# Attention's beginning in an attention-and-two-FFN kernel: other queues, other engines and another place in the order for loads, casts, sums and scalings, and zero products tied to real ones

## The chip, the cores and the metric

The kernel runs on one core of one Trainium2 chip. The metric is the device time of one execution in microseconds (us); the time before is the median of three runs. The engines are TensorE (PE; its weight loads are listed as PEld), VectorE (DVE), ScalarE (ACT), GpSimd (POOL) and SyncE (SP, which only issues DMAs here). ACT issues some DMAs too. Each engine takes its instructions strictly in the order of its own queue, so an instruction that waits holds up all that stands behind it on that engine.

## What is computed

Three stages follow one another; the output of one is the input of the next.

```python
# 1. attention, q, k, v: (2 batches, 8 heads, 576 positions, 64)
q_d, k_d, v_d = means over groups of 4 positions          # "pooled", 144 positions
out_up    = repeat(softmax(scale * q_d @ k_d.T) @ v_d, 4)
out_local = softmax(where(|i - j| < 4, scale * q @ k.T, -1e9)) @ v
x = (out_up + out_local), as 1152 tokens x 512
# 2. a feed-forward layer: softplus(x @ w_in) @ w_out, inner width 2048
# 3. eight experts of inner width 1024, all of them for all tokens, weighted by a gate
#    whose softmax is normalised over tokens and experts eight times
```

The change touches stage 1, most of all its first 45 us.

## The kernel before, in words

**Data.** Two heads lie in one tile of 128 partitions, a *pair*; a batch has four pairs. q of a pair lies in a tile with two halves, in which the other head's rows are blanked with zeros (`blank`), so that one product of 128 rows serves one head. Batch 0's q tiles are called q0a (pairs 0 and 1) and q0b (pairs 2 and 3). v is loaded twice: `vr`, the whole v of a batch in two parts of 640 KB, to be summed in groups of four into `vd`; and `vw`, a window of 122 positions for each tile of 116 queries.

**Units.** Attention is a list of 36 units of four steps (s1 to s4). There are 16 *pooled* units (batch, half, head pair): s1 makes the scores `pd` from sums of q (`qd`, made on DVE, L249) and sums of k (`kd`, POOL L255 and L257, scaled on ACT L258), takes the maximum `nm` on DVE (L286) and the exponentials `e` on ACT (L289); s2 transposes (`ptd`, copied by ACT); s3 multiplies with `vd` (`pvd`) and divides on DVE; s4 transposes back (`pxd`). Each pooled unit of one kind needs the pairs 0 and 1, of the other kind the pairs 2 and 3. There are 20 *local* units (batch, query tile, half of the heads): s1 adds the mask (a product with a bf16 identity, L355) and the scores of q with the scaled k (`pl`, L363), s2 `ptl`, s3 `pvl`, s4 `pxl`; then DVE adds the pooled result (`xf`, L405) and POOL splits it into x (L418, L419).

**Order.** `emit` (L739) writes out the units in one list. With unit n's s1 it writes s2 of unit n-2, s3 of unit n-4 and s4 of unit n-6. Units 0 to 3 are pooled; 4 to 11 alternate local and pooled; 12 to 15 are local; then the second batch comes in. The dictionary `at` hangs other work in front of a unit: loads of batch 1 before unit 1, its v and the first weights before unit 9, its sums before units 11 to 14, and `prep` of the first weight tiles before units 14, 18, 23 and 29. `prep` turns weights given as 64-bit numbers into two 32-bit parts; one takes three passes over 128x1024 on ACT (L123, L125, L130), six on DVE (L126 to L134) and one product on POOL (L136). The weights' buffers (`raw`, two of them) are the ones in which `vr` lies first.

**Who sets the order on an engine.** The framework's planner turns this program into one queue per engine: of the instructions that it believes ready, it takes the one that stands first in the program. An instruction with no input is ready at once and so floats ahead. `tc.issue_after(ins)` holds what is traced inside the block behind `ins`, on the engine of `ins` alone, and it is an order in the queue, not a wait.

**Zero products.** `warm` (L194) issues products of a blanked tile, `pz`, whose result nobody reads: WARM = 17 at the start, then one after each of the first 19 steps, and one after each fourth step up to the 84th, 53 in all.

**Lines to follow.** Loads of q and k L239 and L243 (q of batch 0 on ACT's queue, all else on SP's); identity and mask L91 and L96, their casts L93 and L97; `vr` L273, its sums L276 and L278 (batch 0 on DVE, batch 1 on POOL); scaling of k L259; weights L107.

Of the kernel before, what the change touches and what calls it, by code (L numbers as in the profile page):

```python
# [21 lines left out]
P = 128  # L22
POOLF = 4
G = S // POOLF
GH = G // 2
# [26 lines left out]
WARM, JALL, JN, NJ = 17, 20, 4, 88  # L52
# [23 lines left out]
class Net:  # L76
# [10 lines left out]

    def constants(self):
        nc = self.nc
        self.ident = self.const.tile([P, P], F32, name="ident")  # L90
        nc.sync.dma_start(out=self.ident, in_=self.a["ident"])  # L91
        self.identb = self.atp.tile([P, P], BF16, tag="identb", name="identb", bufs=1)
        nc.vector.tensor_copy(self.identb, self.ident)  # L93
        self.mask = self.atp.tile([P, len(OFF), KW], BF16, tag="mask", name="mask", bufs=1)
        self.maskf = self.convp.tile([P, len(OFF), KW], F32, tag="cm", name="maskf", bufs=1)
        nc.sync.dma_start(out=self.maskf, in_=self.a["mask"])  # L96
        nc.vector.tensor_copy(self.mask, self.maskf)  # L97
        self.ones = self.const.tile([P, P], F32, name="ones")
        nc.gpsimd.memset(self.ones, 1.0)
# [105 lines left out]
    def attention_pools(self, stack):  # L205
        tc = self.tc
        self.convp = stack.enter_context(tc.tile_pool(name="conv", bufs=1, side="right"))
        self.qkp = stack.enter_context(tc.tile_pool(name="qkp", bufs=NPAIR, side="right"))
        self.vwp = stack.enter_context(tc.tile_pool(name="vwp", bufs=3, side="right"))
        self.atp = stack.enter_context(tc.tile_pool(name="atp", bufs=3, side="right"))  # L210
        self.tmp = stack.enter_context(tc.tile_pool(name="tmp", bufs=2, side="right"))
        self.psm = stack.enter_context(tc.tile_pool(name="psm", bufs=2, space=bass.MemoryType.PSUM))
        self.psa = stack.enter_context(tc.tile_pool(name="psa", bufs=6, space=bass.MemoryType.PSUM))
        self.kT, self.qd, self.kd, self.vw, self.vd, self.upT = {}, {}, {}, {}, {}, {}

    def places(self):


        q = self.hp.tile([P, 2, 2, S], F32, tag="h", name="q0a")
        x = self.xyp.tile([P, 2, 2, S], F32, tag="xy", name="q0b")  # L220
        self.qT = {(0, p): (q, x)[p // 2][:, p % 2] for p in range(NPAIR)}
        for t in (q, x):
            self.blank(t, self.nc.vector)
# [5 lines left out]
    def load_qk(self, b, p):  # L229
# [11 lines left out]
        for g in range(2):  # L241
            rows = slice(g * D, (g + 1) * D)
            (nc.scalar if b == 0 else nc.sync).dma_start(out=self.qT[b, p][rows, g], in_=self.a["q"][b, p][rows])  # L243

    def pool_qk(self, b, p):
# [11 lines left out]
        nc.gpsimd.tensor_tensor(kd, s[:, :, 0], s[:, :, 1], ALU.add)  # L257
        nc.scalar.activation(kd, kd, AF.Copy, scale=SCALE / (POOLF * POOLF))  # L258
        nc.scalar.activation(k, k, AF.Copy, scale=SCALE)  # L259
        self.qd[b, p], self.kd[b, p] = qd, kd  # L260

# [5 lines left out]
    def load_vd(self, b):  # L267
# [3 lines left out]
        for hf in range(2):  # L271
            r = self.rawp.tile([GP, POOLF, DM], F32, tag="raw", name=f"vr{b}{hf}")
            nc.sync.dma_start(out=r, in_=self.a["vp"][b, hf].rearrange("p (f d) -> p f d", f=POOLF))  # L273
            s = self.convp.tile([GH, 2, DM], F32, tag=("ch", "cs")[hf], name=f"vs{b}{hf}", bufs=1)
# [4 lines left out]
        self.vd[b] = vd  # L279
        self.upT[b] = self.atp.tile([P, NPAIR, G], F32, tag="upT", name=f"upT{b}", bufs=2)  # L280

    def softmax_exp(self, ps, n, m, k, tag):

        nc = self.nc
        nm = self.atp.tile([m, n], F32, tag="nm" + tag, name="nm")
        nc.vector.tensor_reduce(out=nm, in_=ps, op=ALU.max, axis=AX.X, negate=True)  # L286
        e = self.atp.tile([m, n, k], F32, tag="e" + tag, name="e", bufs=3 if tag == "l" else 2)
        for j in range(n):
            nc.scalar.activation(e[:, j], ps[:, j], AF.Exp, bias=nm[:, j : j + 1])  # L289
        return e  # L290

    def pooled(self, b, hf, p):
# [4 lines left out]
        def s1():  # L297
            ps = self.psa.tile([P, 512], F32, tag="a", name="pd")[:GH, : 2 * G].rearrange("p (j k) -> p j k", j=2)
            for j in range(2):
                nc.tensor.matmul(  # L300
# [8 lines left out]
        def s2():  # L309
# [3 lines left out]
            for j in range(2):  # L313
                for kh in range(2):
                    nc.tensor.transpose(ps[:, j, kh], st["e"][:, j, kh * GH : (kh + 1) * GH], ident[:GH, :GH])
# [4 lines left out]
        def s3():  # L320
            ps = self.psa.tile([P, 512], F32, tag="a", name="pvd")[:GH, : 2 * DA].rearrange("p (j d) -> p j d", j=2)
            for j in range(2):
                for kh in range(2):
                    nc.tensor.matmul(
# [14 lines left out]
        def s4():  # L339
            ps = self.psa.tile([P, 512], F32, tag="a", name="pxd")[:, :GH]  # L340
            nc.tensor.transpose(ps, st["ul"].rearrange("p j d -> p (j d)"), ident[:GH, :GH])
# [4 lines left out]
    def local(self, b, t, g):  # L346
# [6 lines left out]
        def s1():  # L353
            ps = self.psa.tile([P, 512], F32, tag="a", name="pl")[:nq, : 4 * KW].rearrange("p (j k) -> p j k", j=4)
            nc.tensor.matmul(  # L355
# [6 lines left out]
            for j in range(4):  # L362
                nc.tensor.matmul(  # L363
# [8 lines left out]
        def s2():  # L372
            ps = self.psa.tile([P, 512], F32, tag="a", name="ptl")[:KW, : 4 * nq].rearrange("p (j q) -> p j q", j=4)
            for j in range(4):
                nc.tensor.transpose(ps[:, j], st["e"][:, j], ident[:nq, :nq])  # L375
# [4 lines left out]
        def s3():  # L380
            ps = self.psa.tile([P, 512], F32, tag="a", name="pvl")[:nq, : 4 * DA].rearrange("p (j d) -> p j d", j=4)
            for j in range(4):
                nc.tensor.matmul(  # L383
# [12 lines left out]
        def s4():  # L396
            ps = self.psa.tile([P, 512], F32, tag="a", name="pxl")[:, : 2 * nq].rearrange("p (j q) -> p j q", j=2)
            for j in range(2):
                nc.tensor.transpose(
# [314 lines left out]
    def run(self):  # L714
# [13 lines left out]
        self.load_qk(0, 1)  # L728
        self.pool_qk(0, 0)
        self.pool_qk(0, 1)  # L730
        for p in (2, 3):
            self.load_qk(0, p)
            self.pool_qk(0, p)
        self.constants()
# [4 lines left out]
        def emit(items, rest):  # L739
# [4 lines left out]
            for it in [*items, *tail]:  # L744
# [5 lines left out]
                for k, u in enumerate(live[::STEP]):  # L750
                    if u is not None:
                        u[k]()
                        n += 1
                        if n < JALL or n % JN == 0 and n < NJ:
                            self.warm(1)
# [11 lines left out]
        def load_rest():  # L767
            self.load_vd(1)
            self.load_raw(1)
# [9 lines left out]
        at = {1: [load_second], 9: [load_rest]}  # L779
        for p in range(NPAIR):  # L780
            at.setdefault(11 + p, []).append(lambda p=p: self.pool_qk(1, p))
        for n, lag, u in zip(range(2 * NFT), (1, 1, 0, 0), (14, 18, 23, 29)):
# [212 lines left out]
```

## Time and profile before

| | us |
|---|---|
| median of three runs | 1072.9 (1071.02 to 1073.95) |
| span of the profiled execution, first to last instruction | 1069.6 |
| TensorE busy in the span | 1048.9 (98%) |
| VectorE busy | 784.1 (73%) |
| ScalarE busy | 435.1 (41%) |
| GpSimd busy | 170.3 (16%) |

Of the profiled execution the page gives no other time than its span. How to read it: a product's busy time contains its way through the array, so products that follow one another overlap in time, and a stretch in which PE is "busy" can be one in which little is done; the distance from one end to the next says more. The granted clock is the share of 2.4 GHz at which PE ran; 0.5 is 1.2 GHz. In a timeline, the bracket behind a row is the idle time of the engine before it and what ended it.

### The profile page before, as it was taken

To read this page: it belongs to the slowest core of one execution; us is meant where nothing else is said; L and a number is where in the kernel's file an instruction comes from. 1 tells how busy PE (TensorE), PEld (TensorE's weight loads), DVE (VectorE), ACT (ScalarE), POOL (GpSimd) and SP (SyncE) were. 2 spreads that over 40 slices of the span, in tenths; PEclk is the share of its full clock that TensorE was granted. 3 is DMA by queue.
4 is the path that set the end of the run, shared out by engine and by line. 5 is a ranking of instruction groups with operands and counts; after the bars stand their busy time and mean duration, and the time that the engine had idled before them with its cause. 6 is when DMAs were issued, how large, how long until landed. Compare 5 with 4: busy or idle time off the path is not lost.

```text
span 1069.6 us, 16125 instructions
## 1 busy us (share of the span) xinstructions
PE 1048.9 (98%) x6421; PEld 961.4 (90%) x6421; DVE 784.1 (73%) x1466; ACT 435.1 (41%) x815; POOL 170.3 (16%) x218
## 2 busy tenths in 40 slices
PE   7899999999999999999999999999999999999998
PEld 4899999999998899898989989898998989899896
DVE  6798799999987697784947658484765848576572
ACT  4787687766743433141413314141331414133130
POOL 3555300002012220211202011120201112020000
PEclk9899999999999999999999999999999999999999
DMA  9541032222111221111211111121111112110003
GB/s 262 165 136 61 2 119 79 79 79 79 41 40 40 79 80 40 40 41 40 79 40 40 41 40 40 40 80 40 40 40 40 41 40 79 40 40 1 1 2 88
DMA packets 13035, 63.99 MB, mean 60 GB/s; under 512 B 1760, under 2 KB 2016, under 8 KB 6496
## 3 DMA queue, kind: packets, MB, share of 16 engines
q1 hardware_dynamic: 12320, 61.79, 17.7%
q10 hardware_dynamic: 640, 1.18, 0.4%
q8 instruction: 50, 0.82, 0.3%
q14 instruction: 25, 0.20, 0.1%
HBM read 60.60 MB, written 2.36 MB: 59 GB/s over the span
## 4 chain that ended last, share of the span: by engine, by line
PE 87%; DVE 4%; ACT 3%; POOL 1%; issue 0%; ACTq 0%; DVEq 0%
PE po L585 37%; PE pu L536 32%; PE ph L443 8%; PE py L485 7%; PE pvl L383 1%; PE pl L363 0%; ACT cm L125 0%; ACT e L454 0%; DVE ch L129 0%; POOL x L418 0%; ACT r L457 0%; DVE a L167 0%; PE ptl L375 0%; ACT e L453 0%; PE pg L634 0%
## 5 line engine op out<-in xcount | busy, mean ns | idle before, releaser
L536 PE MATMUL pu<-T,a 128*128 128x320 f32 (+1 forms) x2688 | 354.1, 293 | 1.2 <-DVE yp L497 1.2
L536 PEld LDWEIGHTS pu<-T,a 128*128 128x128 f32 x2688 | 351.2, 188 | 2.7 <-issue 1.4
L585 PE MATMUL po<-w,h 128*128 128x512 f32 x960 | 225.3, 394 | 0.0
L607 DVE SCALAR_TENSOR_TENSOR acc<-po,prob,acc 128x512 f32<-128x512 f32 x126 | 94.1, 749 | 176.8 <-PE po L585 176.8
L585 PEld LDWEIGHTS po<-w,h 128*128 128x128 f32 x960 | 180.0, 188 | 41.3
L187 ACT CAST w<-raw 128x1024 fp32r<-128x1024 f32 x32 | 33.3, 1049 | 274.9 <-PE po L585 274.9
L585 PE MATMUL po<-w,h0a 128*128 128x512 f32 x576 | 142.4, 391 | 0.6 <-DVE w L188 0.6
L156 POOL TENSOR_TENSOR s<-raw 128x256 f32<-128x256 f32 x32 | 29.1, 909 | 679.5 <-DVE a L167 476.2
L585 PEld LDWEIGHTS po<-w,h0a 128*128 128x128 f32 x576 | 107.3, 188 | 22.5 <-DVE w L188 1.0
L443 PE MATMUL ph<-x,w 128*128 128x384 f32 x576 | 104.5, 337 | 1.3 <-ACT yp L495 1.3
L485 PE MATMUL py<-h,w 128*128 128x384 f32 x576 | 104.5, 338 | 1.2 <-DVE h L464 0.9
L485 PEld LDWEIGHTS py<-h,w 128*128 128x128 f32 x576 | 100.5, 188 | 1.9 <-DVE h L464 1.3
L443 PEld LDWEIGHTS ph<-x,w 128*128 128x128 f32 x576 | 100.1, 188 | 1.6 <-ACT yp L495 1.6
L548 ACT ACTIVATE h<-c 128x320 fp32r<-128x320 f32 x128 | 58.6, 469 | 79.9 <-DVE c L559 79.9
L549 DVE SCALAR_TENSOR_TENSOR h<-c,h 128x320 fp32r<-128x320 f32 x128 | 68.0, 539 | 0.3
L559 DVE TENSOR_TENSOR c<-v,pu 128x256 f32<-128x256 f32 (+1 forms) x128 | 57.7, 450 | 10.8 <-PE pu L536 7.9
L548 ACT ACTIVATE h0a<-c 128x256 fp32r<-128x256 f32 x96 | 37.4, 417 | 50.2 <-DVE c L559 50.1
L188 DVE TENSOR_TENSOR w<-raw,w 128x1024 fp32r<-128x1024 f32 x32 | 39.0, 1220 | 22.4 <-ACT w L187 22.4
L585 PE MATMUL po<-w,h0b 128*128 128x512 f32 x192 | 54.4, 390 | 0.0
L585 PEld LDWEIGHTS po<-w,h0b 128*128 128x128 f32 x192 | 36.0, 188 | 7.5
L557 ACT COPY p<-pu 128x256 f32<-128x256 f32 (+1 forms) x64 | 25.1, 393 | 37.4 <-PE pu L536 36.1
L549 DVE SCALAR_TENSOR_TENSOR h0a<-c,h0a 128x256 fp32r<-128x256 f32 x96 | 39.0, 419 | 0.9 <-ACT h0a L548 0.6
(141 smaller groups left out, 1249.3 us busy)
## 6 DMA issues: line engine op xcount, KB each, us to landing
raw<-in_w SPq DMA_DIRECT2D x48, 1024.0 KB, 4.9
vw<-in_vw SPq DMA_DIRECT2D x10, 260.0 KB, 2.8
vr<-in_vp SPq DMA_DIRECT2D x4, 640.0 KB, 8.6
k<-in_k SPq DMA_DIRECT2D x8, 288.0 KB, 5.4
out<-acc SPq DMA_DIRECT2D x5, 256.0 KB, 2.0
q<-in_q SPq DMA_DIRECT2D x8, 144.0 KB, 5.3
out<-acc SPq DMA_DIRECT2D x8, 128.0 KB, 2.3
q0a<-in_q ACTq DMA_DIRECT2D x4, 144.0 KB, 5.2
```

Of the source, the lines that this page charges most:

```text
L156: nc.gpsimd.tensor_tensor(s[:, 0], a21, a22, ALU.add)
L187: nc.scalar.copy(w[:, 0], raw)
L188: nc.vector.tensor_tensor(w[:, 1], raw, split(w[:, 0]), ALU.subtract)
L443: nc.tensor.matmul(ps[:, i], lhsT=wv[:, a, k, fo : fo + P], rhs=x[:, b, k], start=(n == 0), stop=(n == 3 * KD - 1),)
L485: nc.tensor.matmul(ps[:, a], lhsT=w[:, i, d * P : (d + 1) * P], rhs=h[:, j, f], start=(n == 0), stop=(n == 3 * NFT - 1),)
L536: nc.tensor.matmul(ps, lhsT=w[:, x, a, k], rhs=t[:, y, b, k], start=(m == 0), stop=(m == 5))
L548: act = nc.scalar.activation(hi, src, AF.Relu)
L549: dve = nc.vector.scalar_tensor_tensor(lo, src, 0.0, split(hi), ALU.max, ALU.subtract)
L557: nc.scalar.copy(to, ps)
L559: nc.vector.tensor_tensor(to, src, ps, ALU.add)
L585: nc.tensor.matmul(ps, lhsT=self.h[s, i, f][:, at * P : (at + 1) * P], rhs=w[:, j], start=(n == 0), stop=(n == 3 * NFT - 1),)
L607: nc.vector.scalar_tensor_tensor(acc, ps, pe, acc, ALU.mult, ALU.add)
```

## The change

- Loads: in the order of use. q of pair 0 stays on ACT's queue, q of the pairs 1 to 3 moves to SP's. The identity is loaded after pair 1, the mask after pair 3.
- The blanking of q0b moves from DVE to POOL, and so do the two casts to bf16 (identity, mask); these casts and the blanking of `ones` stand behind POOL's sum of k of pair 1.
- `pool_qk` of batch 0's pairs 2 and 3 moves behind the maximum (on DVE) and the exponentials (on ACT) of unit 1. The scaling of k is a function of its own, `scale_k`; batch 0's four come behind these exponentials too.
- The sums of v of batch 0 move behind the maximum of unit 3 (`sum_vd`, before unit 4).
- WARM goes from 17 to 22; each of the other 36 zero products is queued behind the real product or transpose that precedes it in the program.
- The first two `prep` move from units 14 and 18 to 16 and 19.

```diff
 STEP = 2
-WARM, JALL, JN, NJ = 17, 20, 4, 88
+WARM, JALL, JN, NJ = 22, 20, 4, 88
 GP = 80
...
+    def load_ident(self):
+        self.ident = self.const.tile([P, P], F32, name="ident")
+        self.nc.sync.dma_start(out=self.ident, in_=self.a["ident"])
+
+    def load_mask(self):
+        self.maskf = self.convp.tile([P, len(OFF), KW], F32, tag="cm", name="maskf", bufs=1)
+        self.nc.sync.dma_start(out=self.maskf, in_=self.a["mask"])
+
     def constants(self):
         nc = self.nc
-        self.ident = self.const.tile([P, P], F32, name="ident")
-        nc.sync.dma_start(out=self.ident, in_=self.a["ident"])
         self.identb = self.atp.tile([P, P], BF16, tag="identb", name="identb", bufs=1)
-        nc.vector.tensor_copy(self.identb, self.ident)
+        nc.gpsimd.tensor_copy(self.identb, self.ident)
         self.mask = self.atp.tile([P, len(OFF), KW], BF16, tag="mask", name="mask", bufs=1)
-        self.maskf = self.convp.tile([P, len(OFF), KW], F32, tag="cm", name="maskf", bufs=1)
-        nc.sync.dma_start(out=self.maskf, in_=self.a["mask"])
-        nc.vector.tensor_copy(self.mask, self.maskf)
+        nc.gpsimd.tensor_copy(self.mask, self.maskf)
         self.ones = self.const.tile([P, P], F32, name="ones")
...
         self.psa = stack.enter_context(tc.tile_pool(name="psa", bufs=6, space=bass.MemoryType.PSUM))
-        self.kT, self.qd, self.kd, self.vw, self.vd, self.upT = {}, {}, {}, {}, {}, {}
+        self.kT, self.qd, self.kd, self.vw, self.vd, self.upT, self.vr = {}, {}, {}, {}, {}, {}, {}
...
         self.qT = {(0, p): (q, x)[p // 2][:, p % 2] for p in range(NPAIR)}
-        for t in (q, x):
-            self.blank(t, self.nc.vector)
+        for t, engine in ((q, self.nc.vector), (x, self.nc.gpsimd)):
+            self.blank(t, engine)
...
             rows = slice(g * D, (g + 1) * D)
-            (nc.scalar if b == 0 else nc.sync).dma_start(out=self.qT[b, p][rows, g], in_=self.a["q"][b, p][rows])
+            (nc.scalar if b == p == 0 else nc.sync).dma_start(out=self.qT[b, p][rows, g], in_=self.a["q"][b, p][rows])
...
         kd = self.atp.tile([P, G], F32, tag="kd", name=f"kd{b}{p}", bufs=NPAIR)
-        nc.gpsimd.tensor_tensor(kd, s[:, :, 0], s[:, :, 1], ALU.add)
+        self.pooled_k = nc.gpsimd.tensor_tensor(kd, s[:, :, 0], s[:, :, 1], ALU.add)
         nc.scalar.activation(kd, kd, AF.Copy, scale=SCALE / (POOLF * POOLF))
-        nc.scalar.activation(k, k, AF.Copy, scale=SCALE)
         self.qd[b, p], self.kd[b, p] = qd, kd
+
+    def scale_k(self, b, p):
+        k = self.kT[b, p]
+        self.nc.scalar.activation(k, k, AF.Copy, scale=SCALE)
...
             nc.sync.dma_start(out=r, in_=self.a["vp"][b, hf].rearrange("p (f d) -> p f d", f=POOLF))
+            self.vr[hf] = r
+        self.vd[b] = vd
+        self.upT[b] = self.atp.tile([P, NPAIR, G], F32, tag="upT", name=f"upT{b}", bufs=2)
+
+    def sum_vd(self, b):
+        nc, vd = self.nc, self.vd[b]
+        for hf in range(2):
+            r = self.vr[hf]
             s = self.convp.tile([GH, 2, DM], F32, tag=("ch", "cs")[hf], name=f"vs{b}{hf}", bufs=1)
...
             e.tensor_tensor(vd[:, hf, :, 0:D], sv[:, 0], sv[:, 1], ALU.add)
-        self.vd[b] = vd
-        self.upT[b] = self.atp.tile([P, NPAIR, G], F32, tag="upT", name=f"upT{b}", bufs=2)
...
         nm = self.atp.tile([m, n], F32, tag="nm" + tag, name="nm")
-        nc.vector.tensor_reduce(out=nm, in_=ps, op=ALU.max, axis=AX.X, negate=True)
+        self.top = nc.vector.tensor_reduce(out=nm, in_=ps, op=ALU.max, axis=AX.X, negate=True)
         e = self.atp.tile([m, n, k], F32, tag="e" + tag, name="e", bufs=3 if tag == "l" else 2)
         for j in range(n):
-            nc.scalar.activation(e[:, j], ps[:, j], AF.Exp, bias=nm[:, j : j + 1])
+            self.exp = nc.scalar.activation(e[:, j], ps[:, j], AF.Exp, bias=nm[:, j : j + 1])
         return e
...
-                nc.tensor.matmul(
+                self.pe = nc.tensor.matmul(
...
         self.load_qk(0, 1)
+        self.load_ident()
+        self.load_qk(0, 2)
+        self.load_qk(0, 3)
+        self.load_mask()
         self.pool_qk(0, 0)
         self.pool_qk(0, 1)
-        for p in (2, 3):
-            self.load_qk(0, p)
-            self.pool_qk(0, p)
-        self.constants()
+        with self.tc.issue_after(self.pooled_k.ins):
+            self.constants()
         self.load_vd(0)
...
                         if n < JALL or n % JN == 0 and n < NJ:
-                            self.warm(1)
+                            with self.tc.issue_after(self.pe.ins):
+                                self.warm(1)
...
             self.load_vd(1)
+            self.sum_vd(1)
             self.load_raw(1)
...
-        at = {1: [load_second], 9: [load_rest]}
+        def pool_rest():
+            with self.tc.issue_after(self.top.ins), self.tc.issue_after(self.exp.ins):
+                self.pool_qk(0, 2)
+                self.pool_qk(0, 3)
+                for p in range(NPAIR):
+                    self.scale_k(0, p)
+
+        def sum_first():
+            with self.tc.issue_after(self.top.ins):
+                self.sum_vd(0)
+
+        at = {1: [load_second], 2: [pool_rest], 4: [sum_first], 9: [load_rest]}
         for p in range(NPAIR):
-            at.setdefault(11 + p, []).append(lambda p=p: self.pool_qk(1, p))
-        for n, lag, u in zip(range(2 * NFT), (1, 1, 0, 0), (14, 18, 23, 29)):
+            at.setdefault(11 + p, []).extend(
+                (lambda p=p: self.pool_qk(1, p), lambda p=p: self.scale_k(1, p))
+            )
+        for n, lag, u in zip(range(2 * NFT), (1, 1, 0, 0), (16, 19, 23, 29)):
             at.setdefault(u, []).append(lambda n=n, lag=lag: prep(n, lag))
```

## Rows read from the trace of the kernel before

**Rows 1.** The page's heading and part 1: busy time, share, instructions

```profile
span 1069.6 us, 16125 instructions
PE 1048.9 (98%) x6421; PEld 961.4 (90%) x6421; DVE 784.1 (73%) x1466; ACT 435.1 (41%) x815; POOL 170.3 (16%) x218
```

**Rows 2.** Windows: busy PE, PEld, DVE, ACT, POOL; granted clock, DMA share, GB/s

```profile
10.00:20.00 10.00, 6.73 (x43) 4.07 (x43) 6.82 (x10) 3.38 (x10) 0.95 (x3) 1.00 1.03 280
...
24.00:41.00 17.00, 16.36 (x169) 15.74 (x168) 13.03 (x35) 11.60 (x40) 10.87 (x12) 0.96 0.84 247
41.00:50.00 9.00, 6.54 (x42) 6.20 (x41) 5.15 (x14) 7.24 (x19) 1.50 (x3) 0.62 0.13 49
50.00:100.00 50.00, 46.42 (x416) 44.33 (x416) 46.83 (x120) 41.11 (x110) 30.48 (x28) 1.00 0.36 117
...
320.00:1069.60 749.60, 744.35 (x4384) 670.51 (x4383) 503.04 (x1002) 217.04 (x418) 93.58 (x120) 1.00 0.13 45
```

**Rows 3.** Windows, zero products pz alone: busy PE, their number, clock, DMA

```profile
8.00:24.00 16.00, 8.15 (x28) 0.93 1.05 276
24.00:70.00 46.00, 0.00 (x0) 0.91 0.53 165
70.00:76.00 6.00, 0.77 (x2) 1.00 0.16 44
```

**Rows 4.** Timeline of DVE, 11 to 23 us: start, length, line, instruction, idle before

```profile
11.07 0.35 DVE L97 CAST mask<-maskf 128x366 bf16<-128x366 f32 x1 [0.40 <-DMA maskf<-in_mask]
11.51 1.35 DVE L249 TENSOR_REDUCE qd<-q0b 128x288 f32<-128x1152 f32 x1
12.78 0.81 DVE L286 TENSOR_REDUCE nm<-pd 72x2 f32<-72x288 f32 x2
...
18.19 1.22 DVE L276 TENSOR_TENSOR vs<-vr 72x1024 f32<-72x1024 f32 x1 [1.90 <-DMA vr<-in_vp]
19.33 1.34 DVE L249 TENSOR_REDUCE qd<-q0b 128x288 f32<-128x1152 f32 x1
20.59 0.68 DVE L278 TENSOR_TENSOR vd<-vs 72x512 f32<-72x512 f32 x1
...
21.77 0.81 DVE L286 TENSOR_REDUCE nm<-pd 72x2 f32<-72x288 f32 x2
```

**Rows 5.** Timeline of PE, 15 to 27 us

```profile
15.95 1.46 PE L203 MATMUL pz<-z 128*128 128x512 bf16 x6
...
20.73 0.71 PE L300 MATMUL pd<-kd,qd 128*72 128x144 f32 x4 [3.31 <-DVE qd L249]
...
23.96 1.16 PE L324 MATMUL pvd<-vd,ptds 72*72 72x65 f32 x8
...
24.92 0.82 PE L300 MATMUL pd<-kd,qd 128*72 128x144 f32 x4
...
25.82 0.68 PE L324 MATMUL pvd<-vd,ptds 72*72 72x65 f32 x8
```

**Rows 6.** Timeline, 34 to 54 us: the first weights, ScalarE's wait, the products behind it

```profile
34.57 2.66 SPq L107 DMA_DIRECT2D raw<-in_w  x2
...
37.98 0.22 ACT L342 COPY upT<-pxd 128x72 f32<-128x72 f32 x1
...
40.88 1.12 ACT L125 ACTIVATE cm<-raw 128x1024 f32<-128x1024 f32 x1 [2.69 <-DMA raw<-in_w]
...
43.62 0.57 PE L355 MATMUL pl<-mask,identb 116*116 116x488 bf16 x1 [2.46 <-ACT e L289]
...
43.98 1.02 PE L363 MATMUL pl<-k,q0a 128*116 128x122 f32 x4
...
50.74 0.58 PE L363 MATMUL pl<-k,q0a 128*116 128x122 f32 x4
...
53.76 0.58 PE L363 MATMUL pl<-k,q0a 128*112 128x122 f32 x4
```

**Rows 7.** Timeline: a GpSimd cast, GpSimd's first sum of batch 1's v, a load's issue

```profile
94.17 3.34 POOL L418 CAST x<-xf 128x232 fp32r<-128x232 f32 x1 [1.74 <-DVE xf L405]
...
32.19 4.67 POOL L276 TENSOR_TENSOR vs<-vr 72x1024 f32<-72x1024 f32 x2 [1.07 <-DVE qd L249]
...
6.80 0.47 ACTq L243 DMA_DIRECT2D q0b<-in_q  x1
```

**Rows 8.** One line each: length min/median/max in ns, first and last start

```profile
L418 POOL CAST x<-xf x24: 243/376/3339, 39.7 to 127.5; 128x232 fp32r<-128x232 f32 x12, 128x224 fp32r<-128x224 f32 x4, 128x72 fp32r<-128x72 f32 x2, 128x160 fp32r<-128x160 f32 x2
L227 POOL MEMSET q<- x8: 571/572/572, 1.1 to 5.4; 64x576 f32 x8
```

More of the change, by code (lines that the diff above doesn't have):

```diff
@@ L314, in s2 @@
                 for kh in range(2):
-                    nc.tensor.transpose(ps[:, j, kh], st["e"][:, j, kh * GH : (kh + 1) * GH], ident[:GH, :GH])
+                    self.pe = nc.tensor.transpose(ps[:, j, kh], st["e"][:, j, kh * GH : (kh + 1) * GH], ident[:GH, :GH])
             pt = self.atp.tile([GH, 2, 2, GH], F32, tag="ptd", name="ptds")
@@ L323, in s3 @@
                 for kh in range(2):
-                    nc.tensor.matmul(
+                    self.pe = nc.tensor.matmul(
                         ps[:, j],
@@ L340, in s4 @@
             ps = self.psa.tile([P, 512], F32, tag="a", name="pxd")[:, :GH]
-            nc.tensor.transpose(ps, st["ul"].rearrange("p j d -> p (j d)"), ident[:GH, :GH])
+            self.pe = nc.tensor.transpose(ps, st["ul"].rearrange("p j d -> p (j d)"), ident[:GH, :GH])
             nc.scalar.copy(self.upT[b][:, p, hf * GH : (hf + 1) * GH], ps)
@@ L354, in s1 @@
             ps = self.psa.tile([P, 512], F32, tag="a", name="pl")[:nq, : 4 * KW].rearrange("p (j k) -> p j k", j=4)
-            nc.tensor.matmul(
+            self.pe = nc.tensor.matmul(
                 ps,
@@ L362, in s1 @@
             for j in range(4):
-                nc.tensor.matmul(
+                self.pe = nc.tensor.matmul(
                     ps[:, j],
@@ L374, in s2 @@
             for j in range(4):
-                nc.tensor.transpose(ps[:, j], st["e"][:, j], ident[:nq, :nq])
+                self.pe = nc.tensor.transpose(ps[:, j], st["e"][:, j], ident[:nq, :nq])
             pt = self.atp.tile([KW, 4, nq], F32, tag="ptl", name="ptls")
@@ L382, in s3 @@
             for j in range(4):
-                nc.tensor.matmul(
+                self.pe = nc.tensor.matmul(
                     ps[:, j], lhsT=st["pt"][:, j], rhs=self.vw[b, t][:KW, 4 * g + j], start=True, stop=True
@@ L398, in s4 @@
             for j in range(2):
-                nc.tensor.transpose(
+                self.pe = nc.tensor.transpose(
                     ps[:, j], st["ul"][:, 2 * j : 2 * j + 2].rearrange("p j d -> p (j d)"), ident[:nq, :nq]
```

## Prediction

> **What bounds the kernel now.** I read the busy times first, then the windows, then the timelines of the stretches where PE stands idle. The span is PE's: 98% busy, and from 320 us on 744 of 750 us [rows 1, 2]. Nothing of the change lies there. The windows show where time without real products can still lie: 10 to 20 us, where PE's busy 6.73 us are largely zero products while DMA is saturated (share 1.03, 280 GB/s); then 41 to 50 us, where PE is busy 6.54 of 9 us at a mean granted clock of 0.62. From 24 to 41 us only 0.64 us of PE are idle, from 50 to 100 us 3.6, and there DVE has 46.8 of 50 us filled [rows 2]. So after the start PE is the bound, and each thing put into its queue costs what it takes, unless a wait swallows it.
>
> The start's chain stands in DVE's timeline: the first maxima (nm) come at 12.78, behind the mask's cast and a sum of q of pair 2; the sum of pair 3 comes only at 19.33, behind a sum of v that waited 1.90 us for its load; the second maxima follow at 21.77 [rows 4]. On PE the scores of pair 3 wait for it 3.31 us, till 20.73, and the first pvd starts at 23.96; from there PE runs closely [rows 5]. The stop at 41 us is ACT's: it waits 2.69 us for the first weights, the exponentials stand behind, PE waits 2.46 us and goes on at 1.2 GHz: four pl take 1.02 us, and 0.58 us later at 2.4 GHz [rows 6].
>
> **The change, part by part.**
>
> 1. **q's sums ahead of v's.** Pair 3's sum (1.34 us) [rows 4] no longer stands behind a sum of v; maxima, exponentials and transposes of the first four units are then done before `vd` is. What is late next is `vd` itself: the same loads (four k, eight q, identity, mask, two parts of v; 3.8 MB by their shapes) stand ahead of v's second part, and DMA was saturated, so it still lands at about 18.1. Behind it 1.22 us of sum and 0.68 of the next make 20.1 [rows 4], and the first pvd follows: 23.96 - 20.1 = 3.9 us earlier. The other vs and vd stand in DVE's queue in front of the first local maxima; that wait of DVE is the old one without the 1.34 us. I add 0.6 us for products that PE can put ahead of vd (one group of pd, some transposes, at the distances of [rows 5]): **-4.5**. Bounds: -1.3 (vd's own gain, the sum of q gone from between) and -6 (the first scores of a local unit, 1.0 us as two groups of 0.58 that overlap [rows 6], done ahead too).
>
> 2. **Clock at the start.** From 24 to 41 us the clock is 0.96, so some 1.4 us are at 1.2 GHz, and the first pvd takes 1.16 us against 0.68 later [rows 2, 5]. With no long wait in front: **-0.5** (bounds -0.7 and 0).
>
> 3. **Zero products.** The trace has 28 of them between 8 and 24 us, none from 24 to 70, two after [rows 3]: without inputs they floated ahead and filled waits. One costs (1.46 - 0.38)/5 = 0.217 us of PE [rows 3, 5], 0.38 being the length of one, 0.77/2. Tied, they stand behind their steps. Steps 9 to 19 come after the first pvd (it is step 9), that is 11, and of the 17 later ones 15 are new there: 26 x 0.217 = 5.6 us at most. The waits left hide some: 0.64 us in 24 to 41 us, and a part of the 3.6 us in 50 to 100 us [rows 2]. I take 18 of them before 41 us less 0.64, that is 3.3, and 0.4 after: **+3.7** (bounds 0, if all fall in waits, and 5.6). WARM's five more replace those that used to float to the start; they lie in the wait for the first loads and cost nothing; if the first scores came earlier than they end, 1.1 us.
>
> 4. **prep two units later.** The first weights' buffers are v's of batch 1: their load is issued at 34.57, behind GpSimd's first sum of it at 32.19 (two sums, 4.67 us), and ACT gets them at 40.88 [rows 6, 7]. All this hangs on saturated DMA and does not move. ACT came to the place at 38.2 [rows 6]. By parts 1 to 3 (zero products with the 3.3 us that fall before) it comes 1.7 us earlier, 36.5, and two local units later: 50.74 to 53.76, 3.0 us each [rows 6], so at 42.5. The load has landed: PE's 2.5 us of wait go, and with them the low clock. At 0.62 over 9 us 6.8 us were at 1.2 GHz [rows 2]; some 5 us of that had products, half is lost: 2.4 us. **-4.9** (bounds -5.4, with ACT's smaller waits, and +1.7, if ACT stops at the same place and waits for the same landing: then what was won before is used up).
>
> 5. **Moves of queues and engines.** Six issues of q, 0.47 us each [rows 7], go from ACT to SP; SP then has 12 issues ahead of v's, some 5.6 us, before anything but DMA's own pace decides: 0 (bounds 0 and +0.5). The two blankings on GpSimd take about 2 x 1.14 us, from 0.57 us for half the width [rows 8], ahead of its sums of k; covered by vd, which comes later in any case; without that cover 2.3 us. ACT's four scalings of k stand behind the exponentials of unit 1 and in front of the first pl; hidden by the same cover: 0 (bounds 0 and +1). The mask is loaded after pair 3, and GpSimd waits for it with the casts in front of what comes next on its queue, sums of k of batch 1, needed far later: 0. A GpSimd cast has a median of 0.38 us but took 3.34 us in the stretch where DVE is full [rows 7, 8]; that would put the first pl 3.0 us later, still before vd's 20.1. The Trainium skill (SBUF — State Buffer, Who interferes with whom) says more sharply that a DVE operation with two SBUF inputs and a GpSimd one that reads SBUF block each other wholly, and a tensor_reduce never does, so a cast beside v's sums would wait for a whole sum; by that rule this part would be +1, by the rows' cover 0, and the row of 3.34 us agrees with it as far as one row can.
>
> 6. **Given back later.** DVE is 94% full from 50 to 100 us [rows 2], and its work on the weights can't begin before they land. At 41 us attention is ahead by 1.7 us, so PE's gain above that must come from DVE's slack of 3.2 us in 50 to 100 and 3.9 in 41 to 50. I take back **+2.1** (bounds 0 and 4.9, all of part 4).
>
> Sum: -4.5 - 0.5 + 3.7 - 4.9 + 0 + 2.1 = **-4.1 us**. Against the profiled span of 1069.6 [rows 1] this is 1065.5; the runs' median is 3.3 us above that span, and I keep the distance: **1068.8 us**, 0.4% less. About 0.3% (3.2 us) is what a measurement of this kernel can tell from no change.
>
> **Rivals.**
>
> *The landing pins everything (no change).* The planner places ACT's work on the weights where it believes them landed, not where the program has unit 16; if that is the same place relative to attention, ACT waits for the same landing at 40.88 and PE's gain is gone by 43.6. For it: the landing is DMA's, and a tie orders, it doesn't wait. Against: the program's order decides among what is ready, and units 14 and 15 now come first. Left is parts 1 to 3 absorbed, plus the zero products after unit 13, 10 less two old ones, 1.7 us at most, partly in waits: +0.6, 1073.5 us.
>
> *Zero products cost more than the start gains (slower).* Place: PE's queue behind steps 9 to 84; price 5.6 us by part 3. It decides, with ACT's wait kept at its old length, once the first pvd comes later than 23.96 - (5.6 - 3.2) = 21.6 us. With the start at its lower bound (-1.3): +4.3, 1077.2 us. For it: the closeness of PE from 24 us on. Against: 2.5 + 3.6 us of waits in which they can lie.
>
> *The start doesn't move*, because GpSimd, now with blankings, casts and sums of k in one queue, holds up the sums of k of pairs 2 and 3: vd covers it unless it is over 5 us; then parts 1 and 2 fall away and the sum is +0.9, 1073.8 us.
>
> **Chances.** Forecast 0.52, landing 0.27, start unmoved 0.06, zero products 0.15. The forecast's own range is 1064.5 to 1070.5: parts 1 and 6 at their better ends below, 3 and 6 towards their worse ends above. The whole range goes on to 1074.0, to take in both cases of no change; above it lie the slower rival and little else. Faster by over 0.3%: 0.50 (the forecast, less its upper end, and a little of the landing's case with a shorter wait); the same 0.34; slower 0.16.
>
> **What would show it.** Step 1: nm of units 0 and 1 before 11 us, the sum of pair 3 before the sums of v, pvd first at about 20. Step 2: clock 1.0 from 20 to 41 us. Step 3: some 26 pz from 20 to 70 us, PE's waits shorter beside them. Step 4: no ACT row that waits over 1 us for the weights, clock 1.0 in 41 to 50 us, first weights' pass at 41 to 43 us. Step 5: GpSimd's mask cast before 16 us. Step 6: DVE still over 90% in 50 to 100 us. I am wrong if ACT waits again for the weights' landing, if pvd does not start before 22 us, or if the time is won or lost after 150 us.

## The result and the profile after

The changed kernel takes **1083.1 us** (median of six, 1080.18 to 1085.9); the kernel before, beside it, 1072.9. The ratio is 1.0103 [1.0084, 1.0122]: 1.0% **slower**, where 0.4% faster was forecast. The profiled execution was the slowest of the six (1085.9), so its spans, 1084.1 against 1069.6, lie 4 us further apart than the medians.

The heading and part 1 of the page, for [rows 1]:

```profile
span 1084.1 us, 16121 instructions
PE 1055.8 (97%) x6426; PEld 968.1 (89%) x6426; DVE 783.0 (72%) x1462; ACT 435.6 (40%) x815; POOL 172.7 (16%) x222
```

PE is busy 7 us more, of a span 14.5 longer; GpSimd, which took over casts and a blanking, is busy 2.4 us more, DVE and ACT as before. The windows, for [rows 2] (columns as there):

```profile
10.00:20.00 10.00, 6.62 (x32) 5.34 (x33) 3.43 (x4) 5.14 (x14) 2.97 (x8) 0.54 1.04 277
24.00:41.00 17.00, 12.48 (x99) 10.91 (x99) 9.90 (x25) 6.46 (x21) 8.49 (x6) 0.80 0.84 228
41.00:50.00 9.00, 7.94 (x45) 6.28 (x45) 1.72 (x5) 7.32 (x20) 1.75 (x4) 0.62 0.17 69
50.00:100.00 50.00, 48.02 (x433) 45.21 (x433) 46.59 (x116) 40.16 (x111) 26.79 (x31) 1.00 0.31 97
100.00:120.00 20.00, 16.80 (x123) 16.07 (x122) 12.44 (x32) 10.38 (x30) 8.26 (x7) 0.83 0.21 67
```

Three things: PE is less busy from 24 to 41 us (12.48 us, before 16.36) and at a lower clock (0.80, before 0.96); DVE has 1.72 us of work in the nine from 41 to 50 (before 5.15 [rows 2]); and 50 to 100 us are full as before, so there is little room to catch up. The zero products, for [rows 3]:

```profile
8.00:24.00 16.00, 2.92 (x6) 0.68 1.04 276
24.00:70.00 46.00, 9.92 (x25) 0.85 0.48 139
```

The start, for [rows 4, 5]: first GpSimd and ACT, then DVE and PE, from the timeline:

```profile
3.01 4.90 POOL L231 MEMSET q<- 64x576 f32 x8
8.01 1.28 POOL L259 TENSOR_TENSOR ks<-k 128x288 f32<-128x288 f32 x2
...
13.07 2.39 ACT L267 ACTIVATE k<-k 128x576 f32<-128x576 f32 x4
...
15.36 0.53 ACT L262 ACTIVATE kd<-kd 128x144 f32<-128x144 f32 x2
...
22.36 0.68 ACT L267 ACTIVATE k<-k 128x576 f32<-128x576 f32 x1 [4.02 <-POOL ks L259]
...
25.10 0.68 ACT L267 ACTIVATE k<-k 128x576 f32<-128x576 f32 x1 [2.06 <-POOL ks L259]
...
25.69 1.16 ACT L302 ACTIVATE e<-pd,nm 72x144 f32<-72x144 f32 x4
```

```profile
10.08 1.02 PE L313 MATMUL pd<-kd,qd 128*72 128x144 f32 x6 [2.69 <-ACT kd L262]
11.13 0.45 DVE L299 TENSOR_REDUCE nm<-pd 72x2 f32<-72x288 f32 x1 [1.71 <-PE pd L313]
...
12.41 2.60 DVE L253 TENSOR_REDUCE qd<-q0b 128x288 f32<-128x1152 f32 x2
...
15.72 0.75 PE L313 MATMUL pd<-kd,qd 128*72 128x144 f32 x2 [3.30 <-ACT kd L262]
...
20.06 0.45 DVE L299 TENSOR_REDUCE nm<-pd 72x2 f32<-72x288 f32 x1 [5.05 <-PE pd L313]
...
26.11 0.72 PE L328 MATMUL ptd<-ident,e 72*72 72x72 f32 x4 [4.18 <-ACT e L302]
...
27.48 0.43 PE L337 MATMUL pvd<-vd,ptds 72*72 72x65 f32 x2
```

q's sums do stand ahead of v's (12.41, both in a row), but the scores come no earlier. Three other waits took the place of the old one: the blankings of batch 1's q, now themselves behind q0b's, stand ahead of GpSimd's first sum of k (8.01, before 6.11); ACT's four scalings of k stand ahead of kd of pairs 2 and 3 (15.36); and batch 1's scalings of k, which wait for GpSimd's sums of the same k and through them for a load, stand ahead of the exponentials of units 2 and 3 (25.69). The first pvd starts at 27.48, 3.5 us **later** than before [rows 5]. Around 40 us, for [rows 6, 7]:

```profile
32.17 2.35 POOL L291 TENSOR_TENSOR vs<-vr 72x1024 f32<-72x1024 f32 x1 [7.10 <-DMA vr<-in_vp]
...
35.94 2.35 POOL L291 TENSOR_TENSOR vs<-vr 72x1024 f32<-72x1024 f32 x1 [1.41 <-DVE qd L253]
...
38.25 2.48 POOL L293 TENSOR_TENSOR vd<-vs 72x512 f32<-72x512 f32 x2
40.70 0.80 POOL L261 TENSOR_TENSOR kd<-ks 128x144 f32<-128x144 f32 x2
41.15 0.32 ACT L262 ACTIVATE kd<-kd 128x144 f32<-128x144 f32 x1 [5.20 <-POOL kd L261]
...
42.06 1.24 PE L313 MATMUL pd<-kd,qd 128*72 128x144 f32 x4 [3.48 <-ACT e L302]
43.13 1.12 ACT L127 ACTIVATE cs<-raw 128x1024 f32<-128x1024 uint32 x1
43.40 0.46 DVE L299 TENSOR_REDUCE nm<-pd 72x2 f32<-72x288 f32 x1 [4.01 <-PE pd L313]
```

The wait of 2.69 us for the first weights is gone (cs at 43.13 waits for nothing). But ACT waits 5.20 us for kd of batch 1's first pairs, with exponentials behind it, PE 3.48 us for these, DVE 4.01. In the trace of before, GpSimd's same sums are done much earlier:

```profile
29.07 0.81 POOL L257 TENSOR_TENSOR kd<-ks 128x144 f32<-128x144 f32 x2 [5.27 <-PE pd L300]
```

There they stand **ahead** of the sums of batch 1's v [rows 7], in the changed kernel behind them. The first part of v lands at 32 us in both, and its sums are 2 x 2.35 + 2.48 = 7.2 us of GpSimd, so what stands behind them cannot run before some 39 us; as the second part's sum starts only at 35.94, it is 40.70. Near 110 us PE stops once more, this time for the fourth weight tile, its clock at 0.83 in that window:

```profile
108.22 2.66 POOL L140 TENSOR_TENSOR w<-cs,ch 128x1024 fp32r<-128x1024 f32 x1
...
110.93 0.69 PE L498 MATMUL py<-h,w 128*128 128x384 f32 x1 [3.11 <-POOL w L140]
```

Read by the end of the same product in both traces, the changed kernel is 5.5 us behind at the 32nd pvd (35.4 us), 14.0 at the 32nd pd (51.1), 8.8 at the 72nd pl (60.5), 9.7 at the 80th pvl (79.2), 14.3 at the 120th pvl (121.0), and from there the distance stays. Of the 14.0, 5.2 come back because the kernel before has its own stop and low clock behind its 32nd pd [rows 6], which the changed one has not. About two thirds of the loss, then, are there once the stop at 42 us is over, and 4.6 us come at the stop near 110. That the second stop follows from the first is not shown: the fourth tile's product starts 9.8 us later than before (98.42), hardly more than PE is late by then.

### The profile page after: what moved, and what is told of

Read it like the earlier page. It is cut to its first block, busy times and chain, and to the rows that moved or that the text cites. A ratio compares the mean times of both kernels' runs of the same rounds, so it can differ in the third digit from the quotient of the medians.

```text
span 1084.1 us, 16121 instructions
## 1 busy us (share of the span) xinstructions
PE 1055.8 (97%) x6426; PEld 968.1 (89%) x6426; DVE 783.0 (72%) x1462; ACT 435.6 (40%) x815; POOL 172.7 (16%) x222
## 4 chain that ended last, share of the span: by engine, by line
PE 86%; DVE 4%; ACT 2%; POOL 1%; issue 0%; DVEq 0%; ACTq 0%
PE po L598 37%; PE pu L549 32%; PE ph L456 8%; PE py L498 7%; PE pvl L396 1%; PE pl L376 1%; DVE ch L133 0%; ACT cm L129 0%; ACT r L470 0%; ACT e L467 0%; DVE cs L137 0%; DVE a L171 0%; ACT w L134 0%; PE pg L647 0%; DVE T L539 0%
```

## The experiments

Each ratio is to the kernel before on the same chip (median 1072.1 to 1073.7). "First pvd" and DVE's work from 10 to 50 us are from the profiles.

| kernel | us | ratio | first pvd, us | DVE 10 to 50, us |
|---|---|---|---|---|
| before | 1072.9 | 1 | 23.96 | 27.58 |
| changed | 1083.1 | 1.0103 [1.0084, 1.0122] | 27.48 | 18.12 |
| e1 loads, casts, blanking | 1067.8 | 0.9951 [0.9937, 0.9965] | 22.34 | 27.21 |
| e2 sums, scalings | 1071.8 | 0.9984 [0.9964, 1.0003] | 21.69 | 29.03 |
| e3 ties | 1079.1 | 1.0059 [1.0038, 1.0081] | 24.48 | 29.87 |
| e4 prep later | 1070.1 | 0.9964 [0.9941, 0.9986] | 25.36 | 27.18 |
| e5 changed, untied | 1073.7 | 1.0013 [1.0002, 1.0023] | 24.10 | 23.05 |
| e6 changed, k before v | 1072.8 | 1.0006 [0.9991, 1.0020] | 27.41 | 24.62 |
| e7 changed, k scaled later | 1083.3 | 1.0107 [1.0088, 1.0126] | 23.64 | 18.24 |
| e8 changed, old sums | 1072.0 | 0.9998 [0.9985, 1.0011] | 23.08 | 26.38 |
| e9 e1 and e4 | 1066.9 | 0.9955 [0.9942, 0.9968] | 22.77 | 28.52 |
| e10 e9, k scaled later | 1069.6 | 0.9981 [0.9966, 0.9995] | 22.83 | 27.85 |
| e11 e5, e6 and e7 | 1070.5 | 0.9990 [0.9973, 1.0006] | 22.43 | 24.07 |
| e12 e6, 17 pz fewer | 1071.7 | 0.9989 [0.9973, 1.0005] | 27.04 | 24.95 |
| e13 changed, start mended | 1080.5 | 1.0079 [1.0059, 1.0099] | 23.11 | 20.56 |
| e14 e13 and e6 | 1075.9 | 1.0039 [1.0025, 1.0053] | 23.10 | 25.79 |
| e15 e1, q blanked later | 1070.9 | 0.9994 [0.9982, 1.0006] | 18.65 | 27.27 |
| e16 e1 again | 1068.1 | 0.9962 [0.9946, 0.9977] | 23.07 | 27.17 |

### Each part alone

**e1**: the kernel before with the loads' order, and the casts and q0b's blanking on GpSimd.

```diff
-        for t in (q, x):
-            self.blank(t, self.nc.vector)
+        for t, engine in ((q, self.nc.vector), (x, self.nc.gpsimd)):
+            self.blank(t, engine)
...
+        self.load_ident()
+        self.load_qk(0, 2)
+        self.load_qk(0, 3)
+        self.load_mask()
```

> The kernel before with the loads' order, the casts and the blanking of q0b on GpSimd alone. Queues theory (the loss comes when batch 1's sums of v on GpSimd, waiting for their load, get ahead of batch 1's sums of k, and ScalarE and TensorE wait for these): here GpSimd keeps the sums of k first, so 1070 to 1076 us. Start theory (GpSimd comes to the first sums of k 2 us late, TensorE stands idle and its clock falls from 10 us on, and that alone is handed on): 1076 to 1081 us. Zero-product theory (the tied products cost 4 to 6 us): no change, 1071 to 1075 us.

Measured: 0.49% faster, below all three forecasts, and 0.38% in e16. The first pd is late (its group ends 2.2 us later), but the 16th pd comes 3.0 us earlier and the first pvd 1.6. GpSimd keeps kd ahead of v. By the ends of the same products, though, only 0.9 us of the profile's gain of 2.7 are there at the 96th py (145 us); 1.6 come right behind it, from a stop that the kernel before has and e1 and e16 have not:

```profile
146.94 8.75 PE L443 MATMUL ph<-x,w 128*128 128x384 f32 x48 [1.30 <-ACT yp L495]
```

Why it goes is not shown.

**e2**: the new places of the sums and scalings alone.

```diff
-        at = {1: [load_second], 9: [load_rest]}
+        at = {1: [load_second], 2: [pool_rest], 4: [sum_first], 9: [load_rest]}
```

> The kernel before with only the new places of the sums of q, the scalings of k and the sums of v. Queues theory: GpSimd keeps batch 1's sums of k ahead of its sums of v, so 1068 to 1075 us. Start theory: the first scores come as before, so the same or faster, 1068 to 1073. Zero-product theory: no loss, 1068 to 1073. My own prediction's first part: 1068.5, since the first pvd comes at about 20 us instead of 24.

The first pvd comes 2.3 us earlier, behind vd; at the end of the profile 0.8 us are left, and the interval holds 1: the 1068.5 of the prediction's first part did not come.

**e3**: WARM = 22 and the tie alone.

```diff
-                            self.warm(1)
+                            with self.tc.issue_after(self.pe.ins):
+                                self.warm(1)
```

> The kernel before with the zero products tied and 22 at the start, nothing else. Zero-product theory: some 26 products of 0.22 us newly on TensorE's path and gaps unfilled: 1076 to 1081 us. Queues theory: hardly any loss, since the other engines' queues stay as they were: 1071 to 1075 us.

0.59% slower, the time of the zero-product theory. But most of the loss isn't where the products stand: behind by 1.9 us at the 72nd pl (54 us) and by 1.4 at the 80th pvl (71 us), the kernel is 5.1 us behind at the 120th pvl (112 us), with a stop of 3.02 us in between. GpSimd, DVE and PE in its timeline:

```profile
99.24 2.65 POOL L136 TENSOR_TENSOR w<-cs,ch 128x1024 fp32r<-128x1024 f32 x1
...
100.19 2.11 DVE L464 TENSOR_TENSOR h<-l,h 128x384 fp32r<-128x384 f32 x1
...
102.36 0.44 PE L485 MATMUL py<-h,w 128*128 128x384 f32 x1 [3.02 <-DVE h L464]
```

DVE's h starts beside GpSimd's product of the weights and ends 0.4 us after it: 2.11 us for what takes 0.54 at its shortest, and PE waits for it. In e4, e5 and e9 h takes 2.0 us in the same way and PE waits only 0.5 us, so a long h alone does not make this stop.

**e4**: `prep` later alone.

```diff
-        for n, lag, u in zip(range(2 * NFT), (1, 1, 0, 0), (14, 18, 23, 29)):
+        for n, lag, u in zip(range(2 * NFT), (1, 1, 0, 0), (16, 19, 23, 29)):
```

> The kernel before with the first two weight tiles prepared before units 16 and 19 instead of 14 and 18. My prediction's part 4 by itself: ScalarE's wait of 2.69 us for the weights and TensorE's 2.46 us behind it go, with the low clock: 1068 to 1071 us. If the planner puts the work where it thinks the weights landed: 1071.5 to 1074.5 us. If VectorE's queue is the bound from 50 to 100 us, later weights cost: 1074 to 1078 us.

0.36% faster, a time inside the first forecast, but not for its reason: ACT still waits for the first weights, 4.38 us, and PE 4.15 us for ACT.

By their ratios times 1073 us the four alone come to -5.3 - 1.7 + 6.3 - 3.9 = **-4.6 us**; together they gave +11.1. What costs is that they meet.

### What meets what

**e5**: the changed kernel with the zero products free again and WARM = 17 (the edit of e3 taken back).

```diff
-WARM, JALL, JN, NJ = 22, 20, 4, 88
+WARM, JALL, JN, NJ = 17, 20, 4, 88
...
-                            with self.tc.issue_after(self.pe.ins):
-                                self.warm(1)
+                            self.warm(1)
```

> The changed kernel with its zero products free again (17 at the start, no ties). If the tie costs what it cost alone (6 us): 1077 us. If the parts add up (loads -5, sums -2, prep -4): 1063 us. Queues theory: here too GpSimd's queue has batch 1's sums of v ahead of its sums of k, but ScalarE's queue has the exponentials ahead of the scalings that wait for them, so most of the loss goes: 1065 to 1073 us.

**e8**: the changed kernel without the new places of sums and scalings (the edit of e2 taken back).

```diff
-        at = {1: [load_second], 2: [pool_rest], 4: [sum_first], 9: [load_rest]}
+        at = {1: [load_second], 9: [load_rest]}
```

> The changed kernel with the sums of q, the scalings of k and the sums of v where they were (so loads, casts, ties and prep changed). If the parts add up: 1073.5 - 5 + 6 - 4 = 1070 us. If it is the new places of sums and scalings together with the ties that makes the loss: also 1068 to 1073. If ties together with the loads' order make it: 1078 to 1084 us.

Either one taken back brings nearly all of the 10 us back (e5, at 1073.7, is just above its third forecast; e8, at 1072.0, fits its first two, which it cannot tell apart). In e5 GpSimd still has v's sums ahead of kd, but they come earlier, and ACT goes on at 37.61:

```profile
37.53 0.82 POOL L261 TENSOR_TENSOR kd<-ks 128x144 f32<-128x144 f32 x2
37.61 1.13 ACT L127 ACTIVATE cs<-raw 128x1024 f32<-128x1024 uint32 x1 [4.34 <-POOL vd L293]
```

So this order does not cost 10 us wherever it stands. **e6** touches neither edit; it puts batch 1's sums of v behind GpSimd's first two sums of k of batch 1. (The load of the first weights moves with them in the program; in both builds it is issued as the first sum of v ends, at 34.55 and 37.10 us.)

```diff
             self.load_vd(1)
-            self.sum_vd(1)
+
+        def sum_second():
+            with self.tc.issue_after(self.pooled_k.ins):
+                self.sum_vd(1)
             self.load_raw(1)
...
+        at[12].append(sum_second)
```

> The changed kernel with batch 1's sums of v on GpSimd behind the sums of k of its pair 1. Queues theory: the scaled sum of k comes at about 35 us instead of 41, TensorE's wait of 3.5 us and the low clock after it go, and VectorE's empty stretch from 39 to 49 us: 1074 to 1079 us. Zero-product theory: 1081 to 1084 us, since 5 us of products and the start stay. Weights come later by some us, which costs at most 2.

10.4 us less than the changed kernel (1.0103 - 1.0006), more than the queues theory forecast, with the first pvd as late as there. GpSimd in its timeline, and its windows:

```profile
33.95 0.81 POOL L261 TENSOR_TENSOR kd<-ks 128x144 f32<-128x144 f32 x2 [8.94 <-ACT upT L355]
34.72 4.67 POOL L291 TENSOR_TENSOR vs<-vr 72x1024 f32<-72x1024 f32 x2
```

```profile
41.00:50.00 9.00, 8.86 (x85) 7.97 (x84) 7.57 (x19) 7.50 (x22) 5.55 (x8) 1.00 0.41 158
```

kd comes at 33.95 instead of 40.70; from 41 to 50 us DVE does 7.57 us of work instead of 1.72, and the clock is 1.00 instead of 0.62. The spans of the two profiles lie 12.7 us apart. By the ends of the same products 6.8 us of that are there at the 80th pvl (72.4 us). 4.2 more come up to the 120th pvl, where PE has no long stop near 100 us in e6:

```profile
101.92 1.68 PE L498 MATMUL py<-h,w 128*128 128x384 f32 x8 [1.27 <-DVE l L475]
```

The last 1.6 are the stop for ACT's yp, which the changed kernel has at 161 us and e6 has not. Only the first 6.8 stand right behind kd.

**e7**: batch 1's scalings of k behind the exponentials, which takes away the last of the three waits at the start.

```diff
-                (lambda p=p: self.pool_qk(1, p), lambda p=p: self.scale_k(1, p))
+                (lambda p=p: self.pool_qk(1, p), lambda p=p: scale_late(p))
```

> The changed kernel with batch 1's scalings of k on ScalarE behind the exponentials of unit 10 and following. ScalarE then does not stand from 18 to 26 us behind loads of batch 1; the exponentials of units 2 and 3 come at about 21.5 instead of 25.7 us. If that delay is handed on: 1078 to 1080 us. If what follows is pinned by the landing of batch 1's v on GpSimd's queue: 1081 to 1084 us.

The first pvd comes 3.8 us earlier, and nothing is won, as the second forecast had it: ACT then waits 8.39 us for kd instead of 5.20, and goes on at 40.30:

```profile
40.30 0.32 ACT L262 ACTIVATE kd<-kd 128x144 f32<-128x144 f32 x1 [8.39 <-POOL kd L261]
```

**e13** takes all three waits away: as e7, with the blankings of batch 1's q behind GpSimd's first two sums of k, and ACT's four scalings behind kd of pairs 2 and 3.

```diff
-            self.blank(q, nc.gpsimd)
+            with self.tc.issue_after(self.pooled_k.ins):
+                self.blank(q, nc.gpsimd)
...
-                for p in range(NPAIR):
-                    self.scale_k(0, p)
+                with self.tc.issue_after(self.scaled_kd.ins):
+                    for p in range(NPAIR):
+                        self.scale_k(0, p)
```

> The changed kernel with the three waits at its start taken away by order: the blankings of batch 1's q on GpSimd behind the first two sums of k, ScalarE's four scalings of k behind the scalings of kd of pairs 2 and 3, and batch 1's scalings of k behind the exponentials. GpSimd's queue still has batch 1's sums of v ahead of kd of its pairs 0 and 1. The theory of GpSimd's queue: the first pvd comes by 22 us instead of 27.5, ScalarE still stops at about 40 us for kd, and the time stays above 1078 us. The rival, that the late start makes the loss: 1068 to 1072 us.

**e14** is e13 with the edit of e6.

> The kernel of the run before, and batch 1's sums of v behind its first two sums of k. The theory of GpSimd's queue: no stop for kd near 40 us, 1069 to 1072 us. If in addition the earlier start is worth its 4.5 us of the prediction's first part: 1067 to 1069 us. If only the start mattered: the same as the run before.

e13 stays at 1080.5 though its start is better than before's (first pvd at 23.11, not yet the 22 that I expected): the late start is not the cause. The order is a part of it: e14 is 4.3 us faster than e13 (1.0079 - 1.0039), not the 10 us of e6, and slower than e6. GpSimd and ACT in the timeline of e13:

```profile
32.63 4.64 POOL L292 TENSOR_TENSOR vs<-vr 72x1024 f32<-72x1024 f32 x2 [8.40 <-DVE rsl L403]
37.23 1.26 POOL L294 TENSOR_TENSOR vd<-vs 72x512 f32<-72x512 f32 x1
38.46 0.80 POOL L262 TENSOR_TENSOR kd<-ks 128x144 f32<-128x144 f32 x2
...
39.85 1.13 ACT L129 ACTIVATE cm<-raw 128x1024 f32<-128x1024 f32 x1 [7.86 <-DMA raw<-in_w]
```

Here ACT's pass over the weights stands ahead of kd in its queue, and waits 7.86 us for their landing; my expectation named the wrong wait, at the right time. e14 keeps a wait of 5.08 us for that landing, and PE's stop for the fourth weight tile, though its DVE did more from 10 to 50 us (25.79 us) than that of e6 (24.62):

```profile
102.58 0.44 PE L499 MATMUL py<-h,w 128*128 128x384 f32 x1 [3.11 <-POOL w L140]
```

The changed kernel, e7, e13 and e14 all have this stop of 3.11 us; e5, e6 and e8 have not. Why the planner places that product so is not shown.

**e11** joins the edits of e5, e6 and e7.

> The changed kernel with untied zero products (alone 1073.7 us), batch 1's sums of v behind its first two sums of k on GpSimd (alone 1072.79 us) and its scalings of k behind the exponentials. The theory of GpSimd's queue: untying and the new order remove the same 10 us, the place of batch 1's sums of k, so together 1070 to 1073 us, not less. The rival, that untying removes some 9 us of zero products from PE's path and the new order another 10 of waiting: about 1064 us.

The two repairs do not add: 1070.5 us, as the first forecast had it, as if they took away the same 10 us. **e12** is e6 without the zero products of the steps 20 to 84.

```diff
-WARM, JALL, JN, NJ = 22, 20, 4, 88
+WARM, JALL, JN, NJ = 22, 20, 4, 20
```

> The changed kernel with batch 1's sums of v behind its first sums of k (1072.79 us), and without the 17 zero products of steps 20 to 84 (NJ = 20). Left out: zero products alone, no part of the result. If they lie on PE's path as the prediction's third part has it: 17 x 0.217 = 3.7 us faster, about 1069 us. If they lie in waits, or VectorE gives the time back later: within 1 us of 1072.8. If they kept the clock up: slower, by some 1 to 2 us.

0.17% less than e6 (0.9989 and 1.0006, the intervals overlap): less than the 3.7 us that 17 products on PE's path would be, though the two intervals do not quite exclude that.

### Towards a better version

**e9**, the edits of e1 and e4:

> The kernel before with two parts of the change: the order of loads and the casts and blankings on GpSimd (alone 1067.75 us), and prep two units later (alone 1070.06 us). If the two parts act in different places (the start; ScalarE's stop at the first weights), they add: about 1073 - 5.3 - 3 = 1064 to 1065 us. If prep's gain is only VectorE's order at 40 to 50 us, which the earlier start has already won: 1067 to 1068 us, as the loads alone. GpSimd's queue keeps batch 1's first two sums of k ahead of its sums of v in this kernel, so the theory of that queue expects no hole in VectorE's work from 40 to 50 us, and no PE wait for ACT kd there.

They don't add: 0.9955, e1 alone 0.9951. ACT's wait for the weights is 0.83 us there, as the prediction's fourth part wanted, and the time is that of e1. **e10**, with the edit of e7 on top:

> The kernel of the run before with batch 1's four scalings of k put behind the exponentials of the unit issued ahead of them. If these scalings stand in front of exponentials that PE waits for: 1 to 2 us faster than that kernel. If what ends the waits is elsewhere (the landing of weights, VectorE): the same within 0.3%.

0.26% slower than e9: against the first forecast, and just inside the second's 0.3%. PE waits 3.13 us for exponentials at 43.91, behind ACT's wait of 3.06 us for the first weights, where e9 has no PE wait over 1 us from 25 to 125 us. **e15**, the loads alone with batch 1's q blanked later (e13's first edit):

> The loads, casts and blankings alone (1067.75 us), with the blankings of batch 1's q behind GpSimd's first two sums of k. The first scores come some 2 us earlier, but in this build's GpSimd queue batch 1's two vs and one vd stand ahead of kd of its pairs 0 and 1. The theory of GpSimd's queue: slower than 1067.75 by 3 us or more, with ScalarE waiting for kd near 40 us, although zero products are untied and the sums stand where they were before. The rival, that the start decides: 1 to 2 us faster.

**e16**, e1 once more beside it:

> The loads, casts and blankings alone, once more, beside the run before on the same chip: 0.995 of the kernel before, 1067 to 1068.5 us.

e16 came as expected. What e15's expectation said of the queue did not hold: kd runs at 24.45, ahead of v. So its time of some 3 us more came by another way. PE and ACT:

```profile
18.65 0.29 PE L338 MATMUL pvd<-vd,ptds 72*72 72x65 f32 x2
...
39.92 1.13 ACT L129 ACTIVATE cm<-raw 128x1024 f32<-128x1024 f32 x1 [5.08 <-DMA raw<-in_w]
```

The first pvd is 5.3 us earlier than before, more than the prediction hoped for. 3.4 us of it are left at the 32nd pd (33.7 us), and 1.5 behind ACT's wait for the first weights (72nd pl, 50.3 us). At the 96th py (144.2 us) e15 is still 1.4 us ahead of the kernel before and 1.1 ahead of e16; then it has the stop of 1.3 us for ACT's yp that the kernel before has and e16 has not. The median is 2.9 us above e16's, but the two profiled executions lie only 0.4 apart, so where the rest goes is not shown. Best are e1 and e9, 0.4 to 0.5% faster than the kernel before and some 1.5% faster than the changed one.

## Why the prediction was wrong

**The step that failed is part 5**, in the sentence that GpSimd's next work, "sums of k of batch 1", is "needed far later: 0". It asked what the moved work waits for, and not in what order GpSimd would then hold two things that wait for different events: kd, for its buffer (freed by a pd of batch 0), and the sums of v, for a landing at 32 us. In the changed kernel they changed places. Put back, they give 10.4 us (e6); of the 12.7 us between the two profiles 6.8 are there soon after this wait, and the rest comes at two later stops of PE, whose tie to the order is not shown. In e14 the same edit gives 4.3. That the late start is not the cause, e7 and e13 show. That the order alone does not do it, and that it takes ties and new sums together, e5 and e8 show; e5 has v ahead of k too, but its ACT goes on at 37.61. What in the planner's picture tips the order was not tried. And with the order put right e6 is still at +0.6 us where -4.1 was forecast, so the other parts missed too:

1. *q's sums ahead, -4.5*: true as an order, and worth 2.3 us at the first pvd in e2; in the changed kernel pvd came at 27.48, past the 22 us that the prediction had named as a sign of being wrong. Two of the three waits part 5 had set to 0 (the blankings; ACT's scalings of batch 0's k, "hidden by the same cover"); the third, batch 1's scalings of k, it did not see, and that one alone is worth 3.8 us at pvd (e7). And a gain there isn't a gain at the end: e15 won 5.3 us at pvd and had 1.4 left at 144 us.
2. *Clock, -0.5*: the wrong sign. From 24 to 41 us, the stretch that it counted, the clock was 0.80 (before 0.96). From 10 to 20 us, with 6 zero products from 8 to 24 us instead of 28 [rows 3], it was 0.54 (before 1.00); in e8, tied too, 11 lie there and it was 1.00.
3. *Zero products, +3.7*: their number was as forecast (25 from 24 to 70 us); alone they cost +6.3 [4.1, 8.7] (e3), about the upper bound of 5.6, and mostly by another way: a stop near 100 us, not their own time in PE's queue. The price for each, 0.217 us, was not confirmed (e12).
4. *prep later, -4.9*: alone -3.9 [-6.3, -1.5], with ACT's wait still there (e4), so not for the reason given. In the changed kernel the wait for the weights went, and what it had cost came back (14.0 us behind at the 32nd pd, 8.8 at the 72nd pl), but the larger one for kd had come at the same place. On top of e1 it is worth nothing (e9).
5. *Moves, 0*: the order of loads and the casts off DVE are the best part of the change (e1 and e16, -4 to -5 us), though little of it shows at the start, and GpSimd's queue is the worst. The mask's cast took 0.49 us beside a tensor_reduce of DVE. The Trainium skill (SBUF — State Buffer, Who interferes with whom) says that a tensor_reduce never blocks GpSimd; the row agrees, and the +1 us that its rule would have made beside v's sums did not arise.
6. *Given back, +2.1*: DVE was 93% full from 50 to 100 us, as forecast. That cut the other way: the loss before it was not made up (8.8 us behind at 60.5 us, 9.7 at 79.2).

Of the rivals, "the landing pins everything" is what e13 and e15 show around 40 us; in the changed kernel itself kd stood in its place. "GpSimd holds up" named the right engine, but other sums, at +0.9 us where the order cost 10. The slower rival was right in sign only.

## What to carry to other kernels

When a change lets a planner lay out its queues anew, list for each in-order engine the neighbours that wait for different events (a landing, a freed buffer), and fix the order of those that can change places; here one such pair, put back, was worth 10 us in one build and 4 in another. A gain ahead of a landing is worth what the landing lets through, so look first for the wait that ends at much the same time whatever comes before it (ACT's wait for the first weights ended at 37 to 44 us in every profile that has one). Measure parts together as well as alone: four that came to -4.6 us gave +11.

## What was unexpected of the hardware

The DVE row of 2.11 us in e3 beside GpSimd's product: it ended 0.4 us after that product (101.89 and 102.30), as if it had stood still for it. It is no single case: in all 13 profiles in which h begins while GpSimd's product of the weights runs, h ends 0.41 or 0.42 us after that product, and takes between 0.80 and 2.11 us, the longer the earlier it began. The same section of the Trainium skill (SBUF — State Buffer, Who interferes with whom) says that a DVE instruction with two SBUF inputs contends with a GpSimd one that reads SBUF, and that the ports they share are an exclusive lock. These rows agree; in e3 PE's stop ended with h (102.36). The prediction had used that rule only for the start, where it cost nothing.
